# Two sums made one type earlier, and four reorderings, in a fused attention and feed-forward kernel

## The chip, the cores and the metric

One core of a Trainium2 chip. The time is the device time of one execution in microseconds; the lower the better. [...]

## The reference

```
q, k, v: (8 batches, 8 heads, 576 positions, 64); w_in: (512, 2048); w_out: (2048, 512)
attention within chunks of 64 positions:
    scores = q_c @ k_c^T / 8;  attn = softmax(scores);  out = attn @ v_c
x = out, as 4608 tokens x 512
h = x @ w_in                       # 4608 x 2048
g = h * tanh(softplus(h))          # "mish"
result = g @ w_out                 # 4608 x 512
```

## The kernel before

The 4608 tokens are 36 tiles of 128, that is 18 pairs of tiles. The first two pairs go through a plain version of the feed-forward part while the weights are read and split. The other sixteen pairs are worked in four rounds `m` = 1 to 4 of four pairs, with a Strassen-Winograd scheme: each product of two matrices, cut in 2 x 2 blocks, is made with seven block products instead of eight, and sums of blocks before and after. While round `m` is worked, the attention of the pairs of round `m` + 1 is done beside it. The whole order of instructions is written out by hand: each engine gets its instructions in the order in which the program emits them and works them in that order; semaphores hold an instruction back until its inputs are there and its output's buffer is free.

In rounds 1 and 2 the product with `w_in` uses the seven-product scheme (`unit`, eight units `u` of two blocks of 128 columns of h; in each unit the steps 0 to 7, behind each of which `beside` may put other work), and the product with `w_out` is the plain one (`down`; its products are held in a list and used as filling between, and in `phase_two` sixteen steps `f` of 12 products each work off the round's second half). In rounds 3 and 4 both products use the scheme.

For that, sums of blocks of w_out are built in round 2: the build of a unit has four steps, `t_whole` (VectorE puts the two parts of w_out together, line 210), `t_sums` (VectorE, three sums, line 219), `t_hi` (ScalarE, upper part, line 223) and `t_lo` (VectorE, lower part, line 227, and then the store to DRAM, which frees the buffer). All builds use one buffer, pool `c_p`, and so do copies of outputs on their way out (`ob_1b`, `ob_2a`, `ob_2b`). `t_keep` stores the blocks that need no sum. The dictionary `BUILDS_OUT` says behind which step of which unit each build step stands.

In rounds 3 and 4, `up_two(m, n)` makes two units at a time, `n` = 0 to 3, with 14 block products each (`product`, six matmuls of 512 columns, line 764), and behind each the function `beside(h)`, `h` = 0 to 13. ScalarE copies a product out of PSUM (lines 996, 1001, 1003), VectorE adds another (line 776), ScalarE applies mish (line 474). The result are the blocks G11, G12, G21, G22 of g for each unit. `s_sums(u)` makes S1 = G21 + G22 and S3 = G11 - G21 on VectorE (lines 943 and 944). Beside it the attention of one pair runs: scores on TensorE (line 271), maximum, difference, exponential, sum, inverse and normalisation on VectorE and ScalarE (lines 297 to 330), transposes on TensorE into PSUM (line 339), a copy of them by ScalarE (line 349), the values' product on TensorE (line 271 again) and its copy (line 360). Scores, transposes and values use one PSUM tile in turn.

`down_all(m)` is the second product: seven types `k` of products, one after the other, each over the eight units:

```
("G11", "W11", "X"), ("G12", "W21", "Y"), ("S2", "T2", "X"), ("S1", "T1", "Z"),
("S3", "T3", "X"), ("S4", "W22", "Z"), ("G22", "T4", "X")
```

The first name is the block of g, the second the block made of w_out, the third the PSUM tiles (two banks each) that take the sum. S2 = S1 - G11 and S4 = G12 - S2. One step, a pair (k, u), is 12 matmuls of 256 columns in `mine` (line 1060): four blocks of 128 tokens times three parts. Two steps ahead of it `operand(k, u)` is emitted: for S2 and S4 first the sum on VectorE (lines 1017 and 1020), in the place of G11 and G12; then the upper part `gh` on ScalarE (line 1024), and the lower part `gl` on VectorE (line 1026), which needs `gh`. `gh` and `gl` have three buffers each. Behind every other step stands one step of the split or sum of the next round's input (`x_step`, lines 415, 416 and 421) in round 3; round 4 has none. Behind a type's last unit the results are copied out of PSUM by ScalarE (`keep`, line 1075) or added by VectorE (`total`, line 1079). At step 1 stand the sums `s_sums` of the last two units, and in round 3 the values' product of the last pair. The blocks of the weights come from DRAM, 256 KB each, eleven in advance (`load_op`, line 751).

Of the kernel before, what the change touches and what calls it, by code (L numbers as in the profile page):

```python
# [14 lines left out]
ALU = mybir.AluOpType  # L15
# [8 lines left out]
def kernel(  # L24
# [22 lines left out]
    nc = tc.nc  # L47
# [5 lines left out]
    NU = NF // 2  # L53
# [338 lines left out]
    def first_pair(m):  # L392
        return PAIRS + 4 * (m - 1)
# [48 lines left out]
    def x_step(m, half, n):  # L442
        step = X_STEPS[n]
        if len(step) == 1:
            x_split(m, half, *step)
        else:
            x_sum(m, half, *step)
# [211 lines left out]
    def slot(s):  # L659
# [52 lines left out]
    BOTH_FROM = 3  # L712
# [11 lines left out]
    TYPES = (  # L724
        ("G11", "W11", "X"),
        ("G12", "W21", "Y"),
        ("S2", "T2", "X"),
        ("S1", "T1", "Z"),
        ("S3", "T3", "X"),
        ("S4", "W22", "Z"),  # L730
        ("G22", "T4", "X"),
    )
# [21 lines left out]
    def next_op():  # L754
        used.append(0)
        return wop[len(used) - 1]
# [29 lines left out]
        ):  # L786
            BUILDS.setdefault(place, []).append((step, n))
    BUILDS_OUT = {}
    for n, (u, h) in enumerate(((1, 0), (2, 0), (3, 0), (4, 0), (4, 4), (5, 0), (6, 0), (7, 0))):
        for i, step in enumerate((t_whole, t_sums, t_hi, t_lo)):  # L790
            BUILDS_OUT.setdefault((u, h + i), []).append((step, n))
        BUILDS_OUT.setdefault((n, 7), []).append((t_keep, n))

    def unit(m, u):
# [99 lines left out]
    def z_of(f):  # L894
        return zb[f // 8][:, f // 2 % 4, f % 2]

    def phase_two(m):
        after = m < QUADS
        p = first_pair(m)
        todo = []  # L900
        if after:
            todo = [lambda n=n: x_step(m + 1, 0, n) for n in range(len(X_STEPS))]
            todo += [lambda: a_raw(first_pair(m + 1) + 3)]
            todo += [lambda n=n: x_step(m + 1, 1, n) for n in range(len(X_STEPS))]
        for f in range(NF):
            d = {}
            if f == 0:
                filled(12)
            g_split(d, z_of(f), f"{m}b_{f}", True)
            if f == 0:  # L910
                for t in range(TOK // P):
                    filled(3)
                    store(f"{m}a", (p, p + 2), t)
            elif after or f < NF - 1:
                filled(12)
            down((m, 1), f, d)
            for _ in range(2):
                if todo:
                    todo.pop(0)()
            if f == 1 and m == 1:  # L920
                a_values(first_pair(m + 1) + 3)
            if f == 10 and m + 1 < QUADS:
                load_qk(first_pair(m + 2))
# [5 lines left out]
    G = {}  # L929
# [11 lines left out]
    def s_sums(u):  # L941
        s1, g11, g21, g22 = (G[u, n] for n in ("S1", "G11", "G21", "G22"))
        nc.vector.tensor_tensor(out=s1, in0=g21, in1=g22, op=ALU.add)
        nc.vector.tensor_tensor(out=g21, in0=g11, in1=g21, op=ALU.subtract)
        G[u, "S3"] = g21

    def up_two(m, n):
        units = (2 * n, 2 * n + 1)
        xt, yt, vt = flip(m)
        j = first_pair(m + 1) + n  # L950
        on = m < QUADS
        x, y, v_ = {}, {}, {}

        def beside(h):
            if h in (1, 2) and n:
                s_sums(2 * n - 3 + h)
            if not on:
                return
            if h == 1:
                a_scores(j)  # L960
                load_v(j)
            elif h == 2:
                a_max(j)
            elif h == 3:
                a_sub(j)
                if n < 3:
                    load_qk(j + 1, pool=(ob_p, "ob"))
            elif h == 4:
                a_exp(j)
            elif h == 6:  # L970
                a_inverse(j)
            elif h == 7:
                a_norm(j)
            elif h == 9:
                a_transpose(j)
                a_copy(j)
            elif h == 11 and n < 3:
                a_values(j)
                a_raw(j)

        for k in range(7):
            for i, u in enumerate(units):
                if k == 0:
                    x[u] = bank(f"x_{m}_{u}", xt[i])
                    z11 = z_new(m, u, "G11")
                    for name in ("G12", "G21", "G22", "S1"):
                        z_new(m, u, name)
                if k == 1:
                    y[u] = bank(f"y_{m}_{u}", yt[i])
                if k == 3:  # L990
                    v_[u] = bank(f"v_{m}_{u}", vt[i])
                o = y[u] if k == 1 else v_[u] if k in (3, 6) else x[u]
                product(k, o, k in (0, 1, 3))
                z = {name: G[u, name] for name in ("G11", "G12", "G21", "G22")}
                if k == 0:
                    nc.scalar.copy(out=z["G11"], in_=o)
                elif k == 1:
                    add(o, z["G11"])
                    mish(z["G11"], z["G11"])
                elif k == 2:  # L1000
                    nc.scalar.copy(out=z["G21"], in_=o)
                elif k == 4:
                    nc.scalar.copy(out=z["G22"], in_=o)  # L1003
                    add(v_[u], z["G22"])
                    mish(z["G22"], z["G22"])
                elif k == 5:
                    mish(z["G12"], o)
                elif k == 6:
                    add(o, z["G21"])
                    mish(z["G21"], z["G21"])  # L1010
                beside(2 * k + i)

    def operand(k, u):
        name = TYPES[k][0]
        if name == "S2":
            G[u, "S2"] = G[u, "G11"]
            nc.vector.tensor_tensor(out=G[u, "S2"], in0=G[u, "S1"], in1=G[u, "G11"], op=ALU.subtract)
        if name == "S4":
            G[u, "S4"] = G[u, "G12"]
            nc.vector.tensor_tensor(out=G[u, "S4"], in0=G[u, "G12"], in1=G[u, "S2"], op=ALU.subtract)  # L1020
        d = {}
        g = G[u, name]
        d["gh"] = ew_l.tile([P, TOK], F32R, name=f"gh_{k}_{u}", tag="gh")
        nc.scalar.copy(out=d["gh"], in_=g)  # L1024
        d["gl"] = ew_l.tile([P, TOK], F32R, name=f"gl_{k}_{u}", tag="gl")
        nc.vector.tensor_tensor(out=d["gl"], in0=g, in1=d["gh"].bitcast(F32), op=ALU.subtract)  # L1026
        return d
# [10 lines left out]
    def down_all(m):  # L1038
# [9 lines left out]
        banks_ = {}  # L1048
        ob = {}
        steps_ = [(k, u) for k in range(len(TYPES)) for u in range(NU)]  # L1050
        ready = [operand(*steps_[0]), operand(*steps_[1])]

        def mine(k, u, d, w_, bs=(0, 1)):
            acc_ = banks_[TYPES[k][2]]
            for t in (t for b in bs for t in (2 * b, 2 * b + 1)):
                o = acc_[t // 2][:, t % 2 * 256 : (t % 2 + 1) * 256]
                for n, (g, part) in enumerate((("gl", 0), ("gh", 1), ("gh", 0))):
                    nc.tensor.matmul(  # L1060
                        o,
                        lhsT=d[g][:, t * P : (t + 1) * P],
                        rhs=w_[:, part],
                        start=(k in (0, 1, 3) and u == 0 and t % 2 == 0 and n == 0),
                        stop=(u == NU - 1 and n == 2),
                        skip_group_check=True,
                    )
# [23 lines left out]
        for i, (k, u) in enumerate(steps_):  # L1091
            if u == 0 and k in (0, 1, 3):
                name = TYPES[k][2]
                banks_[name] = [bank(f"{name}_{m}_{b}", tags[name][b]) for b in range(2)]
            if i == 1:
                for u_ in (NU - 2, NU - 1):
                    s_sums(u_)
            if i + 2 < len(steps_):
                ready.append(operand(*steps_[i + 2]))
            w_ = next_op()  # L1100
            if last and k == len(TYPES) - 1 and u >= NU - 2:
                rest.append((k, u, ready.pop(0), w_))
            else:
                mine(k, u, ready.pop(0), w_)
            load_op()
            if i == 1 and not last:
                a_values(nxt + 3)
            if i % 2 and todo:
                todo.pop(0)()
            if u == NU - 1 and k in ends:  # L1110
                for b in range(2):
                    ends[k](b)
            if (k, u) == (6, 2) and m + 1 < QUADS:
                load_qk(first_pair(m + 2), pool=(ob_p, "ob"))
        ob["C21"] = ob_p.tile([P, 4, 256], F32, name=f"C21_{m}", tag="ob")
        for b in range(2):
            for r in rest:
                mine(*r, (b,))
            o = ob["C21"][:, 2 * b : 2 * b + 2]
# [74 lines left out]
```

## Time and profile before

| | |
|---|---|
| time, median of 3 runs | 892.27 us (892.26 to 895.66) |
| the profiled execution | 893.57 us, its span 891.8 us |
| mean granted clock of TensorE | 0.981 |
| TensorE matmuls busy | 823.5 us (92%) |
| VectorE busy | 525.3 us (59%) |
| ScalarE busy | 437.1 us (49%) |
| DMA, mean | 203 GB/s |

The stages in the profile's time: the first two pairs to about 160 us, round 1 to about 330, round 2 to 520 (its second half from 471), round 3 to 714 (its `down_all` from 614), round 4 to the end (its `down_all` from 791).

In the profile's rows PE is TensorE's matmuls and PEld its weight loads, DVE is VectorE, ACT ScalarE, SP SyncE; "L1026" is line 1026 of the kernel. A row of a timeline gives start and duration in us, engine, line, operation, output<-input, shapes and count, and in brackets the idle time before it on its engine and what ended that. A row of the chain that ended last gives start, duration, and what it was.

### The profile page before, as it was taken

What the parts mean: (1) busy time and instruction counts of PE and PEld (TensorE: products, weight loads), DVE (VectorE), ACT (ScalarE), POOL (GpSimd) and SP (SyncE); (2) the same over time, 40 slices, a digit from 0 to 9 for tenths busy, and PEclk for the clock granted to TensorE, in tenths of its full rate; (3) what the DMA queues carried; (4) which work ended last, traced back from release to release, by engine and by line L of the source; (5) the groups of instructions that cost most, each with busy time, mean ns of one, the idle gap of its engine ahead of it and who ended that gap; (6) DMA issues with size and microseconds to landing.
All of it is one profiled execution on the core that took longest, in us unless ns stands there. A gap on an engine that the chain in (4) does not pass through costs nothing.

```text
span 891.8 us, 15840 instructions
## 1 busy us (share of the span) xinstructions
PE 823.5 (92%) x6300; PEld 693.1 (78%) x6300; DVE 525.3 (59%) x765; ACT 437.1 (49%) x640; POOL 0.7 (0%) x6
## 2 busy tenths in 40 slices
PE   4979988889999999999999999998988999989987
PEld 4757866668888887787788887777878888879887
DVE  6788788556464645647666544455667623345554
ACT  4768766344354534445345435556454344434433
POOL 0000000000000000000000000000000000000000
PEclk9789999999999999999999999999999999989999
DMA  7788766775875306976975069664656676656562
GB/s 271 255 306 307 275 203 214 264 270 204 291 256 155 96 0 179 323 256 233 308 238 165 0 197 306 209 197 136 171 159 170 182 214 191 191 147 179 167 188 61
DMA packets 96440, 181.39 MB, mean 203 GB/s; under 512 B 9072, under 2 KB 29552, under 8 KB 94320
## 3 DMA queue, kind: packets, MB, share of 16 engines
q1 hardware_dynamic: 95936, 179.74, 63.5%
q8 instruction: 50, 0.82, 0.4%
q10 hardware_dynamic: 432, 0.66, 0.3%
q14 instruction: 22, 0.18, 0.1%
HBM read 137.36 MB, written 42.99 MB: 202 GB/s over the span
## 4 chain that ended last, share of the span: by engine, by line
PE 64%; DVE 17%; ACT 9%; DMA 5%; issue 3%; SPq 1%; ACTq 0%; DVEq 0%
PE x L764 15%; PE v L764 8%; PE X L1060 8%; PE y L764 4%; PE Z L1060 3%; DVE gl L1026 3%; ACT gh L1024 2%; DMA wst<-in_w_in 2%; PE av L271 2%; PE Y L1060 2%; DVE wc L132 2%; PE s L271 2%; PE pt L339 2%; PE o_(1, 1)_0_2761 L493 1%; PE o_(2, 1)_0_4421 L493 1%
## 5 line engine op out<-in xcount | busy, mean ns | idle before, releaser
L764 PE MATMUL x<-x_T,w 128*128 128x512 f32 x576 | 144.8, 394 | 5.9 <-ACT zb L868 3.3
L764 PEld LDWEIGHTS x<-x_T,w 128*128 128x128 f32 x576 | 106.1, 188 | 32.3 <-ACT zb L868 4.6
L1024 ACT CAST gh<-G 128x512 fp32r<-128x512 f32 x96 | 58.9, 619 | 96.0 <-PE X L1060 30.6
L1026 DVE TENSOR_TENSOR gl<-G,gh 128x512 fp32r<-128x512 f32 x96 | 65.8, 692 | 59.7 <-ACT gh L1024 58.6
L1060 PE MATMUL X<-w,gh 128*128 128x256 f32 x512 | 95.4, 287 | 0.0
L1060 PE MATMUL X<-w,gl 128*128 128x256 f32 x256 | 75.5, 295 | 14.6 <-DVE gl L1026 14.6
L1060 PEld LDWEIGHTS X<-w,gh 128*128 128x128 f32 x512 | 81.9, 197 | 0.0
L1060 PEld LDWEIGHTS X<-w,gl 128*128 128x128 f32 x256 | 50.3, 196 | 18.1 <-DVE gl L1026 18.1
L776 DVE TENSOR_TENSOR G<-v,G 128x512 f32<-128x512 f32 x32 | 22.1, 691 | 65.8 <-ACT G L1003 34.7
L474 ACT ACTIVATE G<-G 128x512 f32<-128x512 f32 x48 | 30.3, 632 | 59.5 <-DVE G L776 59.5
L461 PE MATMUL h<-x_first,wi 128*128 128x512 f32 (+1 forms) x204 | 50.6, 402 | 0.7 <-ACT x_first L379 0.7
L764 PE MATMUL v<-x_B,w 128*128 128x512 f32 x192 | 48.5, 395 | 2.5 <-DVE zb L776 2.5
L764 PE MATMUL v<-x_T,w 128*128 128x512 f32 x192 | 47.8, 391 | 2.4 <-DVE z L776 1.7
L764 PE MATMUL x<-x_B,w 128*128 128x512 f32 x192 | 48.6, 394 | 0.8 <-DVE x_B L416 0.8
L764 PE MATMUL y<-x_B,w 128*128 128x512 f32 x192 | 49.1, 397 | 0.0
L474 ACT ACTIVATE zb<-zb 128x512 f32<-128x512 f32 x32 | 20.2, 632 | 57.2 <-DVE zb L776 57.2
L1060 PE MATMUL Z<-w,gh 128*128 128x256 f32 x256 | 47.9, 287 | 0.0
L461 PEld LDWEIGHTS h<-x_first,wi 128*128 128x128 f32 x204 | 39.4, 207 | 9.0 <-ACT x_first L379 0.9
L1060 PE MATMUL Z<-w,gl 128*128 128x256 f32 x128 | 38.3, 299 | 8.0 <-DVE gl L1026 7.9
L764 PEld LDWEIGHTS v<-x_B,w 128*128 128x128 f32 x192 | 35.4, 188 | 11.6 <-DVE zb L776 4.2
L764 PEld LDWEIGHTS v<-x_T,w 128*128 128x128 f32 x192 | 35.8, 188 | 10.9 <-DVE z L776 2.1
L493 PE MATMUL o<-wo,gh 128*128 128x512 f32 x128 | 42.5, 414 | 0.3 <-DVE wo L153 0.3
(181 smaller groups left out, 1614.6 us busy)
## 6 DMA issues: line engine op xcount, KB each, us to landing
w<-wa SPq DMA_DIRECT2D x224, 256.0 KB, 3.2
w<-wb SPq DMA_DIRECT2D x112, 256.0 KB, 2.8
v<-in_v SPq DMA_DIRECT2D x16, 512.0 KB, 5.9
wa<-a SPq DMA_DIRECT2D x8, 1024.0 KB, 4.1
wb<-t SPq DMA_DIRECT2D x8, 1024.0 KB, 4.5
wst<-in_w_out SPq DMA_DIRECT2D x7, 1024.0 KB, 5.5
wst<-in_w_in SPq DMA_DIRECT2D x6, 1024.0 KB, 6.1
wa<-wi SPq DMA_DIRECT2D x24, 256.0 KB, 3.9
```

Of the source, the lines that this page charges most:

```text
L132: nc.vector.scalar_tensor_tensor(out=c, in0=x, scalar=mask, in1=y, op0=op, op1=ALU.bitwise_or)
L271: nc.tensor.matmul(o[h * CHUNK : (h + 1) * CHUNK, c, t - ts.start, g], lhsT=l[rows, t, 2 * g + h], rhs=r[rows, t, 2 * g + h], start=True, ...
L339: nc.tensor.transpose(out=d["pt", ts.start][:, t - ts.start, g], in_=d["p"][:, t, g].rearrange("p c k -> p (c k)"), identity=ident,)
L461: nc.tensor.matmul(h[:, cols], lhsT=wi[i // 2][:, i % 2, w_, kt], rhs=x[:, x_, kt, cols], start=(n == 0), stop=(n == 3 * NK - 1),)
L474: nc.scalar.activation(out=out_, in_=in_, func=AF.Mish)
L493: nc.tensor.matmul(acc[t], lhsT=g[:, t * P : (t + 1) * P], rhs=wo[:, f, part], start=(f == 0 and n == 0), stop=(f == NF - 1 and n == 2),)
L764: nc.tensor.matmul(o, lhsT=t[:, w_, kt], rhs=x[x_][:, kt], start=(start and i == 0), stop=(i == 5), skip_group_check=not start,)
L776: nc.vector.tensor_tensor(out=z, in0=o, in1=z, op=ALU.add)
L1024: nc.scalar.copy(out=d["gh"], in_=g)
L1026: nc.vector.tensor_tensor(out=d["gl"], in0=g, in1=d["gh"].bitcast(F32), op=ALU.subtract)
L1060: nc.tensor.matmul(o, lhsT=d[g][:, t * P : (t + 1) * P], rhs=w_[:, part], start=(k in (0, 1, 3) and u == 0 and t % 2 == 0 and n == 0), sto ...
```

## The change

Five edits:

- The sums S2 and S4 leave `operand`. S2 of unit u is made behind `operand` of step (1, u), S4 behind that of step (3, u), by the new function `difference`: one type ahead of the type that uses them.
- In `mine`, the three parts become the outer loop and the four blocks of tokens the inner one, and the order of parts changes: first the four upper x lower, then the four upper x upper, last the four products with the lower part `gl`.
- The operands of the first two steps of `down_all` are emitted behind products 10 and 11 of the last pair of units in `up_two`, not at the start of `down_all`; the list `ready` moves out of `down_all` for that.
- In `up_two`, the attention's transposes and their copy move from behind product 9 to behind product 10, the values' product and its copy from 11 to 12.
- In round 2, unit n + 1 has the build of unit n, one in each unit; before, unit 4 had two builds, and units 5 to 7 those of units 5 to 7. The build of unit 7 moves into `phase_two`, steps 6 to 9.

```diff
--- before.py
+++ after.py
@@ -786,9 +786,10 @@
         ):
             BUILDS.setdefault(place, []).append((step, n))
     BUILDS_OUT = {}
-    for n, (u, h) in enumerate(((1, 0), (2, 0), (3, 0), (4, 0), (4, 4), (5, 0), (6, 0), (7, 0))):
-        for i, step in enumerate((t_whole, t_sums, t_hi, t_lo)):
-            BUILDS_OUT.setdefault((u, h + i), []).append((step, n))
+    T_STEPS = (t_whole, t_sums, t_hi, t_lo)
+    for n in range(NU):
+        for i, step in enumerate(T_STEPS if n < NU - 1 else ()):
+            BUILDS_OUT.setdefault((n + 1, i), []).append((step, n))
         BUILDS_OUT.setdefault((n, 7), []).append((t_keep, n))
 
     def unit(m, u):
@@ -917,6 +918,8 @@
             for _ in range(2):
                 if todo:
                     todo.pop(0)()
+            if m == BOTH_FROM - 1 and 0 <= f - 6 < len(T_STEPS):
+                T_STEPS[f - 6](NU - 1)
             if f == 1 and m == 1:
                 a_values(first_pair(m + 1) + 3)
             if f == 10 and m + 1 < QUADS:
@@ -954,6 +957,8 @@
         def beside(h):
             if h in (1, 2) and n:
                 s_sums(2 * n - 3 + h)
+            if h in (10, 11) and n == NU // 2 - 1:
+                ready.append(operand(0, h - 10))
             if not on:
                 return
             if h == 1:
@@ -971,10 +976,10 @@
                 a_inverse(j)
             elif h == 7:
                 a_norm(j)
-            elif h == 9:
+            elif h == 10:
                 a_transpose(j)
                 a_copy(j)
-            elif h == 11 and n < 3:
+            elif h == 12 and n < 3:
                 a_values(j)
                 a_raw(j)
 
@@ -1010,16 +1015,15 @@
                     mish(z["G21"], z["G21"])
                 beside(2 * k + i)
 
+    ready = []
+
+    def difference(u, out_, x, y):
+        G[u, out_] = G[u, "G11" if out_ == "S2" else "G12"]
+        nc.vector.tensor_tensor(out=G[u, out_], in0=G[u, x], in1=G[u, y], op=ALU.subtract)
+
     def operand(k, u):
-        name = TYPES[k][0]
-        if name == "S2":
-            G[u, "S2"] = G[u, "G11"]
-            nc.vector.tensor_tensor(out=G[u, "S2"], in0=G[u, "S1"], in1=G[u, "G11"], op=ALU.subtract)
-        if name == "S4":
-            G[u, "S4"] = G[u, "G12"]
-            nc.vector.tensor_tensor(out=G[u, "S4"], in0=G[u, "G12"], in1=G[u, "S2"], op=ALU.subtract)
         d = {}
-        g = G[u, name]
+        g = G[u, TYPES[k][0]]
         d["gh"] = ew_l.tile([P, TOK], F32R, name=f"gh_{k}_{u}", tag="gh")
         nc.scalar.copy(out=d["gh"], in_=g)
         d["gl"] = ew_l.tile([P, TOK], F32R, name=f"gl_{k}_{u}", tag="gl")
@@ -1048,15 +1052,14 @@
         banks_ = {}
         ob = {}
         steps_ = [(k, u) for k in range(len(TYPES)) for u in range(NU)]
-        ready = [operand(*steps_[0]), operand(*steps_[1])]
 
 
 
         def mine(k, u, d, w_, bs=(0, 1)):
             acc_ = banks_[TYPES[k][2]]
-            for t in (t for b in bs for t in (2 * b, 2 * b + 1)):
-                o = acc_[t // 2][:, t % 2 * 256 : (t % 2 + 1) * 256]
-                for n, (g, part) in enumerate((("gl", 0), ("gh", 1), ("gh", 0))):
+            for n, (g, part) in enumerate((("gh", 1), ("gh", 0), ("gl", 0))):
+                for t in (t for b in bs for t in (2 * b, 2 * b + 1)):
+                    o = acc_[t // 2][:, t % 2 * 256 : (t % 2 + 1) * 256]
                     nc.tensor.matmul(
                         o,
                         lhsT=d[g][:, t * P : (t + 1) * P],
@@ -1097,6 +1100,10 @@
                     s_sums(u_)
             if i + 2 < len(steps_):
                 ready.append(operand(*steps_[i + 2]))
+            if k == 1:
+                difference(u, "S2", "S1", "G11")
+            elif k == 3:
+                difference(u, "S4", "G12", "S2")
             w_ = next_op()
             if last and k == len(TYPES) - 1 and u >= NU - 2:
                 rest.append((k, u, ready.pop(0), w_))
```

## The prediction

> **What bounds the kernel now.** I read the page's busy times first, then the kernel cut into stretches, then the chain of work that ended last from the third round on, and last the queues of VectorE and ScalarE inside the stretches where TensorE waits.
>
> ```profile
> PE 823.5 (92%) x6300; PEld 693.1 (78%) x6300; DVE 525.3 (59%) x765; ACT 437.1 (49%) x640; POOL 0.7 (0%) x6
> ...
> core 0: us, PE busy (x) PEld busy (x) DVE busy (x) ACT busy (x) POOL busy (x), PEclk, DMA share, GB/s
> 628.50:640.10 11.60, 11.60 (x99) 11.60 (x99) 7.86 (x12) 5.68 (x10) 0.00 (x0) 1.00 0.66 183
> 714.04:790.70 76.66, 76.66 (x337) 62.43 (x335) 24.08 (x36) 31.70 (x55) 0.00 (x0) 1.00 0.70 199
> 790.70:805.00 14.30, 11.62 (x74) 11.63 (x75) 8.55 (x13) 5.30 (x10) 0.00 (x0) 0.76 0.39 112
> ```
>
> TensorE is the bound: 92% busy, and in whole stretches (714 to 791 us) never idle, with the DMA share at 0.70 and the clock at 1.00. So a gain can only come from the stretches where TensorE waits. The chain shows where these are:
>
> ```profile
> 611.48 2.73 PE v L764 x12
> ...
> 616.88 3.14 PE X L1060 x24
> 620.01 1.09 PE av L271 x64
> ...
> 660.32 11.52 PE Z L1060 x96
> ...
> 702.52 11.52 PE X L1060 x96
> 714.04 2.75 PE x L764 x12
> ...
> 787.98 2.73 PE v L764 x12
> ...
> 793.38 14.47 PE X L1060 x96
> ...
> 836.10 11.52 PE Z L1060 x96
> ...
> 875.60 11.53 PE X L1060 x96
> ```
>
> These are the two passes of the second product (`down_all`), seven types of 96 products each. An undisturbed type takes 11.52 us, so one product 0.12 us and a step of 12 products 1.44 us; seven types are 80.64 us. The third round's pass runs from the end of the last first product (611.48 + 2.73 = 614.21) to 714.04: 99.83 us, which is 80.64, the attention's 1.09, and 18.1 lost. The fourth's runs from 790.71 to 887.13 (875.60 + 11.53): 96.42 us, 15.8 lost. Inside: at each start 2.67 us in which TensorE does nothing (614.21 to 616.88, 790.71 to 793.38); 2.95 us in the fourth's first type (14.47 instead of 11.52); and in three types each time 616.88 to 660.32 (43.44 - 34.56 - 1.09 = 7.8), 660.32 to 702.52 (42.20 - 34.56 = 7.6), 793.38 to 836.10 (42.72 - 34.56 - 2.95 = 5.2) and 836.10 to 875.60 (39.50 - 34.56 = 4.9). These four, 25.5 us, lie in the third and the sixth type, S2 and S4. Why:
>
> ```profile
> 649.66 0.68 DVE L1017 TENSOR_TENSOR G<-S,G 128x512 f32<-128x512 f32 x1
> 650.46 0.62 ACT L1024 CAST gh<-G 128x512 fp32r<-128x512 f32 x1 [1.52 <-DVE G L1017]
> 651.11 0.69 DVE L1026 TENSOR_TENSOR gl<-G,gh 128x512 fp32r<-128x512 f32 x1 [0.76 <-ACT gh L1024]
> 651.72 0.68 DVE L1017 TENSOR_TENSOR G<-S,G 128x512 f32<-128x512 f32 x1
> 651.86 0.39 PE L1060 MATMUL X<-w,gl 128*128 128x256 f32 x1 [0.97 <-DVE gl L1026]
> ```
>
> The reader is to see a closed ring: the sum on VectorE (649.66), the upper part on ScalarE that waits for it (650.46), the lower part on VectorE that waits for that (651.11), and only then the next sum (651.72). One turn is 651.72 - 649.66 = 2.06 us, above a step's 1.44. VectorE is not full; it waits 0.76 us in each turn.
>
> **Part 1: the sums one type ahead.** 16 sums of 0.68 us per pass move from the third and sixth types into the second and fourth. None is added. The ring breaks: an upper part then waits only for its buffer (three in turn). What is late next is VectorE's queue itself in the types that take the sums, above all in the third round, where it also splits the next round's input.
>
> ```profile
> 629.25 1.31 ACT L1075 COPY P<-X 128x512 f32<-128x512 f32 x2
> 643.15 0.68 DVE L416 TENSOR_TENSOR x_T<-raw,x_T 128x512 fp32r<-128x512 f32 x1
> 643.75 1.28 DVE L1079 TENSOR_TENSOR P<-Y,P 128x512 f32<-128x512 f32 x2
> 644.95 0.68 DVE L1017 TENSOR_TENSOR G<-S,G 128x512 f32<-128x512 f32 x1
> ```
>
> Back to back, three VectorE operations take 644.95 - 643.15 = 1.80 us, 0.60 to 0.61 each though each is listed at 0.68. In the second type of the third round VectorE gets 8 lower parts, 8 sums and 4 input operations, then two totals and the lower part of the third type's third step: 23 x 0.61 = 14.0 us. It starts some 1.8 us into the type, after the two copies (1.31) and one upper part (0.62, less overlap). Ready: 15.8 us from the type's start. Needed, with part 2, two thirds into that step: 10 x 1.44 + 0.96 = 15.36. So some 0.5 us late, and with restart I charge 0.7; at 0.69 us each it is 17.7, so 2.3 late. The fourth type has no totals: 21 x 0.61 + 1.8 = 14.6 against 15.36, nothing (0.9 late at 0.69). The fourth round has no input operations: 19 x 0.61 + 1.8 = 13.4, nothing.
>
> **Part 2: the lower parts' products last.** The same 12 products and 12 weight loads per step, reordered. Gain: a lower part may come 8 x 0.12 = 0.96 us later, and an upper part's buffer is free 0.48 us earlier. Cost: bank and moving operand now alternate otherwise. Rows show no price for it: the 628.50 to 640.10 stretch changes region every three products and bank every six, at 1.00 clock and 11.52 us a type. I charge nothing; the far bounds are under the rivals.
>
> **Part 3: the first splits moved into the last pair.** Two upper and two lower parts go behind products 10 and 11 of the last pair, where ScalarE and VectorE have room (31.70 and 24.08 of 76.66 us in the fourth round). The chain product, addition, mish, upper part, lower part (2.67 us) leaves both starts, and the third step's parts take its place later. Behind it stand the last four sums of S1 and S3 on VectorE:
>
> ```profile
> 617.94 0.68 DVE L943 TENSOR_TENSOR S<-G,G 128x512 f32<-128x512 f32 x1
> 620.60 0.68 DVE L1026 TENSOR_TENSOR gl<-G,gh 128x512 fp32r<-128x512 f32 x1
> ```
>
> Four sums take 2.66 us. From the pass's start the third lower part begins at about 1.95 us (the gap's 2.67 less a lower part's 0.69), the sums follow it, and the fourth is ready at 1.95 + 0.61 + 2.66 + 0.68 = 5.9. TensorE needs it at 3 x 1.44 + 0.96 = 5.28: 0.7 us late in the fourth round, 0.9 with restart. In the third round the attention's 1.09 us and its load gap stand before it, so nothing.
>
> The 2.95 us of the fourth's first type: its 96 products ran while the granted clock was 0.76, right after the 2.67 us gap; the equal gap at 614.21 cost no clock (11.52 us types follow). I take it that the gap brings it and that it goes. [...]
>
> So the third round's pass gains 18.1 - 0.7 = 17.4 us, the fourth's 15.8 - 0.9 = 14.9.
>
> **Part 4: one build per unit (second round).**
>
> ```profile
> 369.92 1.59 PE y L764 x6
> ...
> 403.37 1.60 PE y L764 x6
> ...
> 441.05 1.59 PE y L764 x6
> ...
> 413.78 1.23 DVE L210 TENSOR_TENSOR t<-wo 128x1024 f32<-128x1024 f32 x1 [1.57 <-DMA wb<-t]
> 425.20 1.22 DVE L210 TENSOR_TENSOR t<-wo 128x1024 f32<-128x1024 f32 x1 [4.14 <-DMA wb<-t]
> 415.66 1.67 PE L764 MATMUL v<-x_B,w 128*128 128x512 f32 x6 [1.18 <-DVE zb L776]
> 428.73 1.67 PE L764 MATMUL v<-x_T,w 128*128 128x512 f32 x6 [1.69 <-DVE z L776]
> ```
>
> A build's first step waits for the store of the build before (one buffer), and everything behind it on VectorE waits too, until TensorE does (1.69 at 428.73). Units three and four take 403.37 - 369.92 = 33.45 us, five and six 441.05 - 403.37 = 37.68. With one build each they should take the same: 4.2 gained (2.9 if only the two named waits of TensorE, 1.18 and 1.69, go). The last build moves into the second half, steps 6 to 9:
>
> ```profile
> 491.26 0.69 DVE L483 TENSOR_TENSOR gl_2b<-zb,gh_2b 128x512 fp32r<-128x512 f32 x1 [1.42 <-ACT gh_2b L479]
> 496.70 0.69 DVE L483 TENSOR_TENSOR gl_2b<-zb,gh_2b 128x512 fp32r<-128x512 f32 x1 [0.82 <-ACT gh_2b L479]
> 416.65 1.61 DVE L219 TENSOR_TENSOR t<-t 128x512 f32<-128x512 f32 x3
> ```
>
> There a step is 2.72 us (two in 496.70 - 491.26) with some 0.8 us idle on VectorE. The build adds 1.22, 1.61, 0 and 1.22 us to four steps. Stepping through from 491.26: a lower part and two splits (3 x 0.61), 1.2, a lower part, a split and a sum (3 x 0.61), 1.6, and the lower part of step 8 begins at 497.6 instead of 496.70. There it had some 1.9 us to spare (a step less the upper part before it); it needs 0.69, and now has 1.0. Nothing charged; were that 0.3 us of cover gone, some 0.5. Its store goes to SyncE's queue with its data ready, and the buffer's next user, the output copies at the half's end, comes six steps later. In the second round's units six to eight the builds only change their number.
>
> **Part 5: attention one product later (third round).**
>
> ```profile
> 559.56 1.07 PE L339 MATMUL pt<-ident,p 128*128 128x128 f32 x8 [0.98 <-DVE p L330]
> 560.59 0.57 ACT L1003 COPY G<-x 128x512 f32<-128x512 f32 x1
> 563.49 1.02 PEld L271 LDWEIGHTS av<-ps,v 64*64 64x64 f32 x64 [0.54 <-ACT ps L349]
> ```
>
> The transposes no longer wait 0.98 us, but the product after them needs the bank that the copy at 560.59 empties (to 561.16): it starts at 561.2 instead of 561.74. So 0.5 us per pair, not 1, and about 0.3 at the values' product. Pairs two and three gain 0.8, pair four 0.5 (its values' product lies in the next pass), and pair one, whose transposes did not wait, an estimate of 0.4 to 0.6; less 0.2 for the splits put before the last copy: 2.4 us. Bounds: 0, if the copies only hand the wait on, and 4 x 0.98 = 3.9.
>
> **Sum.** 4.2 + 2.4 + 17.4 + 14.9 = 38.9 us off the profiled execution's 893.57 (span 891.8): 854.7. The median of the runs shown, 892.27, is 1.3 below it; on that level 853.4, and I say 854.
>
> **Rivals.**
> - *The wait only moves.* VectorE's ring forms again where the sums now stand: all 25.5 us stay, 893.57 - 13.4 = 880, some 879 on the median's level. For it: VectorE gets 20 operations in 11.5 us. Against it: no sum stands any more between an upper part and its lower part's step, and the totals above. Its mild form, the 0.69 us bound, adds 1.6 + 0.9: 857.
> - *The clock stays low in the fourth round's first type*: 2.95 more, 857. For it: only one of two gaps lowered it.
> - *The reordered products run slower* (the other side). Place: 2 x 672 = 1344 products. Each has to lose 38.9 / 1344 = 29 ns before the change gains nothing. Price: at the 0.76 clock 96 products took 14.47 us, 31 ns more each, 41 us in all: 895. Against: the 11.52 us types already alternate banks at clock 1.00. [...]
>
> **Chances.** Forecast 0.73; the wait moves 0.12; clock stays 0.10; slower products 0.05, of which 0.02 within 0.5% and 0.03 beyond (about what a measurement of this kernel can tell from no change). All others are faster by over 0.5%: 0.95. Range: down to 850 (nothing of the charged 1.6 us, 2 more from attention), up to 863 (both bounds of VectorE, the clock, no gain in attention). It leaves out the far end of the first rival and the slower products.
>
> **What would show it.** S2 and S4 types of 11.5 us; no idle time before either pass's first product, and a granted clock of 1.00 behind it; TensorE's waits for lower parts, now at every turn of the ring, under 3 us in all and left at the third type of the third round and the fourth step of the fourth; units five and six at 33.5 us; transposes without a wait, the product behind them with about 0.5. Wrong would be me if VectorE's waits for upper parts come back in the second and fourth types, or if undisturbed types take more than 11.52 us.

## The result and the profile after

The changed kernel takes 854.34 us (median; 853.87 to 855.94), the kernel before 893.96 in the same comparison: 0.9555 of its time, 95% interval 0.9519 to 0.9591. The forecast was 854. The profiled execution's span is 852.8 us instead of 891.8, 39.0 less; the sum said 38.9.

In the rows below, `gh` is the upper part of a float32 operand and `gl`, the rest of it, the lower part, both of type `float32r` ("fp32r" in the rows); a product is the sum of lower x upper, upper x lower and upper x upper, added in PSUM.

The page's busy row and the chain of the kernel after (start, duration, what), with two rows of TensorE's timeline for the end of the third round's first product, which the chain leaves out:

```profile
PE 810.4 (95%) x6300; PEld 686.4 (80%) x6300; DVE 521.6 (61%) x765; ACT 436.1 (51%) x640; POOL 0.7 (0%) x6
...
402.76 1.59 PE y L764 x6
...
436.22 1.59 PE y L764 x6
...
515.66 2.72 PE x L764 x12
...
643.71 11.52 PE Z L1063 x96
655.23 11.52 PE X L1063 x96
666.75 11.52 PE Z L1063 x96
678.27 11.52 PE X L1063 x96
689.79 2.75 PE x L764 x12
...
763.71 2.72 PE v L764 x12
766.43 1.45 PE X L1063 x12
...
772.53 6.49 PE X L1063 x52
779.03 11.52 PE Y L1063 x96
...
836.63 11.53 PE X L1063 x96
```

```profile
603.99 2.91 PE L764 MATMUL v<-x_B,w 128*128 128x512 f32 x12
606.73 1.12 PE L1063 MATMUL X<-w,gh 128*128 128x256 f32 x8
```

The types S2 and S4 are now as long as the others, but for 0.3 us at the third round's S2 (11.83 us): from 643.71 on, four types in a row in the third round take 11.52 us each, and from 779.03 on all of the fourth. The second product begins with no gap, at the end of the product before it: at 603.99 + 2.91 = 606.90 in the third round (the row at 606.73 begins 0.17 us ahead of the end of the row before it) and at 766.43 in the fourth. It takes 689.79 - 606.90 = 82.9 us in the third round instead of 99.83 and 848.16 - 766.43 = 81.7 in the fourth instead of 96.42; 80.64 (and 1.09 for the values' product in the third) is the floor. Units five and six of the second round take 436.22 - 402.76 = 33.46 us.

| part | forecast | before | after | gained |
|---|---|---|---|---|
| units five and six, round 2 | 4.2 | 37.68 | 33.46 | 4.2 |
| first product, round 3 (to 614.21 / 606.90) | 2.4 | 93.72 | 91.24 | 2.5 |
| second product, round 3 | 17.4 | 99.83 | 82.89 | 16.9 |
| second product, round 4 | 14.9 | 96.42 | 81.73 | 14.7 |
| all else | 0 | | | 0.7 |

The 93.72 and the 91.24 us begin where the two chains have the round's first products, at 520.49 and 515.66. Of the last row, 0.6 us lie ahead of the fifth unit (403.37 and 402.76), in the part that no edit touches; that part differs by some 5 us between the profiles below (401.33 to 406.23).

### The profile page after: what moved, and what is told of

Its sections match the earlier page's. It is cut to its first block, busy times and chain, and to the rows that moved or that the text cites. A ratio compares the mean times of both kernels' runs of the same rounds, so it can differ in the third digit from the quotient of the medians.

```text
span 852.8 us, 15933 instructions
## 1 busy us (share of the span) xinstructions
PE 810.4 (95%) x6300; PEld 686.4 (80%) x6300; DVE 521.6 (61%) x765; ACT 436.1 (51%) x640; POOL 0.7 (0%) x6
## 4 chain that ended last, share of the span: by engine, by line
PE 76%; DVE 10%; DMA 5%; ACT 5%; issue 2%; SPq 1%; DVEq 0%; ACTq 0%
PE x L764 17%; PE X L1063 9%; PE v L764 9%; PE Z L1063 5%; PE y L764 5%; PE av L271 2%; DMA wst<-in_w_in 2%; PE s L271 2%; PE h L461 2%; PE o L493 2%; PE pt L339 2%; DVE wc L132 1%; PE Y L1063 1%; PE o_(1, 1)_0_2761 L493 1%; PE o_(2, 1)_0_4413 L493 1%
## 5 line engine op out<-in xcount | busy, mean ns | idle before, releaser
L1063 PE MATMUL X<-w,gh 128*128 128x256 f32 x512 | 72.3, 283 | 0.0
L1063 PEld LDWEIGHTS X<-w,gh 128*128 128x128 f32 x512 | 66.3, 192 | 0.2
L1063 PE MATMUL X<-w,gl 128*128 128x256 f32 x256 | 41.8, 284 | 1.3 <-DVE gl L1030 1.2
L764 PEld LDWEIGHTS x<-x_B,w 128*128 128x128 f32 x192 | 35.2, 188 | 8.6 <-DVE x_B L416 1.2
L764 PEld LDWEIGHTS y<-x_B,w 128*128 128x128 f32 x192 | 35.1, 188 | 7.7
L481 DVE CAST gh<-z 128x512 fp32r<-128x512 f32 x40 | 16.9, 423 | 39.7 <-PE o_(2, 0)_3_3328 L493 20.6
```

What stands on the lines that cost most here:

```text
L481: nc.vector.tensor_copy(out=d["gh"], in_=z)
L764: nc.tensor.matmul(o, lhsT=t[:, w_, kt], rhs=x[x_][:, kt], start=(start and i == 0), stop=(i == 5), skip_group_check=not start,)
L1063: nc.tensor.matmul(o, lhsT=d[g][:, t * P : (t + 1) * P], rhs=w_[:, part], start=(k in (0, 1, 3) and u == 0 and t % 2 == 0 and n == 0), sto ...
```

## The experiments

Since that first part varies, each profile is also read from the start of the fifth unit's second product (the chain's row "PE y") to the end of the span. All five edits lie behind it. Each row is one profile.

| kernel | fifth unit | span | from there | against the change |
|---|---|---|---|---|
| before | 403.37 | 891.8 | 488.4 | +38.4 |
| the change | 402.76 | 852.8 | 450.0 | |
| sums_alone | 403.58 | 868.0 | 464.4 | +14.4 |
| all_but_sums | 402.41 | 872.1 | 469.7 | +19.7 |
| old_order | 401.66 | 854.6 | 452.9 | +2.9 |
| late_first_splits | 402.74 | 857.0 | 454.3 | +4.2 |
| first_splits_alone | 402.04 | 884.8 | 482.8 | +32.7 |
| old_builds | 402.29 | 856.5 | 454.2 | +4.2 |
| old_attention | 403.60 | 855.5 | 451.9 | +1.9 |
| banks_in_turn | 406.23 | 856.4 | 450.2 | +0.1 |
| later_last_sums | 401.33 | 849.6 | 448.3 | -1.8 |
| combined | 404.72 | 851.7 | 447.0 | -3.1 |

**sums_alone: the sums one type ahead, nothing else.**

```diff
 # on the kernel before
-        if name == "S2": ... if name == "S4": ...      (in operand)
+            if k == 1:
+                difference(u, "S2", "S1", "G11")
+            elif k == 3:
+                difference(u, "S4", "G12", "S2")
```

> The kernel before, with S2 and S4 made one type ahead and nothing else of the change. Theory (the ring of sum, upper part, lower part caused the 25.5 us in the third and sixth types, and making the sums ahead opens it): these types take 11.5 us each but for a start up to 1.5 us late in the third round's third type, since the lower part is still needed at a step's first product; 2.67 us stay at both starts of the second product, and the fourth round's first type may stay at 14.5 us; in all some 24 us faster, 869 to 871 us. Rival (the sums need the reordered products as well, because VectorE's queue is full in the types that take them): at most 15 us faster, 879 us or more, with waits for lower parts spread over the second and fourth types of the third round.

Measured 869.38 us, 0.9733 of before (0.9683 to 0.9783); 24.0 us less from the fifth unit on. The ring was the cause, and the sums do not need the reordering. Its chain in the fourth round, and two of its stretches with the granted clock (third column from the right):

```profile
779.80 14.47 PE X L1057 x96
...
805.79 11.52 PE X L1057 x96
...
840.35 11.52 PE Z L1057 x96
```

```profile
777.20:779.80 2.60, 0.00 (x0) 0.00 (x0) 1.40 (x3) 1.91 (x4) 0.00 (x0) 0.88 0.61 184
779.80:786.00 6.20, 6.20 (x29) 6.20 (x30) 4.36 (x8) 1.50 (x3) 0.00 (x0) 0.50 0.16 42
```

S2 (805.79) and S4 (840.35) are undisturbed; the gap and the slow first type behind it stay, at a clock of 0.50 for 6 us. In the third round S2 still takes 12.53 us: its start comes 1.0 us late, within the 1.5 that were allowed for it.

**all_but_sums: the change without its sums.**

```diff
 # on the changed kernel
+        if name == "S2": ... if name == "S4": ...      (in operand again)
-            if k == 1: difference(...)  elif k == 3: difference(...)
```

> The changed kernel, with the sums S2 and S4 back in front of the upper part two steps ahead; all else of the change stays. Theory: the ring is back, one turn of 2.06 us (2.66 with an input operation) against a step of 1.44; the reordered products give back some 0.96 us in each of the four types that have it; the third and sixth types take 15 to 18 us each, and the kernel is 21 to 25 us slower than the changed one: 876 to 880 us. Rival (the reordering of products alone hides most of the ring): under 10 us slower, below 865 us.

Measured 875.05 us, 0.9792 (0.9741 to 0.9843), and 19.7 us more than the change from the fifth unit on: the theory's side, a little under its range. The ring comes back, but the reordering makes it cheaper by more than the 0.96 us per type that I gave it: its chain

```profile
620.01 6.73 PE Y L1070 x56
647.49 1.70 PE X L1070 x12
649.19 11.52 PE Z L1070 x96
```

has S2 from 631.53 (620.01 + 11.52) to 649.19, 17.7 us, 6.1 lost where the kernel before, from 641.46 to 660.32, lost 7.3. That is 1.2 us less. TensorE now waits there for the upper part, not the lower one (from 600 to 700 us, 4.6 us in six waits for `gh` in the types on X, 0.5 in one for `gl`); that the earlier release of its buffer (0.48 us) makes up the rest is argued, not shown.

**old_order: the change with the old order of products in a step.**

```diff
-            for n, (g, part) in enumerate((("gh", 1), ("gh", 0), ("gl", 0))):
-                for t in (...):
+            for t in (...):
+                for n, (g, part) in enumerate((("gl", 0), ("gh", 1), ("gh", 0))):
```

> The changed kernel, with the products of a step in the old order (block of tokens outside; lower, upper x lower, upper x upper inside). Theory: the new order gives each lower part 0.96 us, which is used only where VectorE is late: the fourth step of either round's first type and the start of the third round's third type; each of these waits becomes some 0.96 us longer, 2.9 us in all: 857 us. An undisturbed type takes 11.52 us in both orders. Rival one: the order matters at every step (the later release of an upper part's buffer makes ScalarE late): 5 us or more slower, 860 us. Rival two: the new order costs TensorE something itself; then undisturbed types are shorter than 11.52 us here.

Measured 857.29 us, 0.959 (0.9549 to 0.9632), 2.9 us more from the fifth unit on: as forecast in sum. TensorE's waits in the third round, fourth step and third type, in its timeline:

```profile
612.77 0.39 PE L1063 MATMUL X<-w,gl 128*128 128x256 f32 x1 [1.42 <-DVE gl L1030]
635.38 0.39 PE L1063 MATMUL X<-w,gl 128*128 128x256 f32 x1 [0.76 <-DVE gl L1030]
```

In the changed kernel the first is 0.41 and the second too short to be listed; the one at the fourth round's fourth step is 1.56 us here and 0.83 there. The parts were not quite as forecast: both first types grow by 1.0 us, the third round's third type by only 0.7, and its fifth type, for which nothing was forecast, by 0.3. Undisturbed types are 11.52 us here too, so the new order costs TensorE nothing.

**late_first_splits and first_splits_alone: the first two operands at the start again, and only this part of the change.**

```diff
 # late_first_splits, on the changed kernel (first_splits_alone: the reverse, on the kernel before)
-            if h in (10, 11) and n == NU // 2 - 1:
-                ready.append(operand(0, h - 10))
+        ready.extend(operand(*s) for s in steps_[:2])      # in down_all
```

> The changed kernel, with the first two operands emitted at the start of the second product, as before. Theory: TensorE waits at both starts for addition, mish and upper part, some 2.0 us each (no longer for the lower part), in return the fourth step's waits (0.6 and 0.8 us) mostly go, since the chain ahead of them is the same; 2.5 to 3 us slower, and if a gap of 2 us lets the granted clock fall, up to 3 us more in the first type after it: 857 to 860 us. Rival (the start's wait was hidden anyway by later waits): within 1 us of the changed kernel.

> The kernel before, with the first two operands behind products 10 and 11 of the last pair and nothing else of the change. Theory (the 2.67 us gap at the start of the fourth round's second product lets the granted clock fall): no gap at either start, and the fourth round's first type shows a clock of 1.00 and loses nothing but a wait of some 1.8 us at its fourth step (the lower part is still needed first); some 6 us faster than before, 886 to 888 us, the ring in the third and sixth types unchanged. Rival (the clock falls for another reason, at that time or place): the first type still takes 14 us or more besides that wait.

The first: 858.55 us, 0.9597 (0.9555 to 0.964), and 4.2 us more from the fifth unit on. These are two gaps of 1.95 us and one fall of the clock, 1.5 us (the third round's first type takes 14.55 us; in the kernel before, with no fall there, 13.06), less the two waits at the fourth step, which are gone. Its stretches at both starts:

```profile
606.80:608.80 2.00, 0.09 (x1) 0.00 (x0) 0.69 (x1) 1.27 (x4) 0.00 (x0) 1.00 0.60 189
608.80:613.50 4.70, 4.66 (x28) 4.49 (x32) 4.61 (x8) 2.79 (x5) 0.00 (x0) 0.64 0.27 81
769.40:771.40 2.00, 0.06 (x1) 0.00 (x0) 0.70 (x2) 1.27 (x4) 0.00 (x0) 1.00 0.74 186
771.40:776.00 4.60, 4.59 (x38) 4.59 (x39) 4.53 (x8) 2.70 (x5) 0.00 (x0) 1.00 0.35 95
```

Two equal gaps: behind the third round's the clock falls to 0.64, behind the fourth's it stays at 1.00. In the kernel before it was the other way round, 1.00 behind the third round's (616.90 to 620.00) and 0.53 behind the fourth's (793.40 to 800.00); why was not shown. The second kernel, a single run, took 886.55 us, 5.7 us less than before from the fifth unit on, as forecast. Its fourth round:

```profile
788.00:802.00 14.00, 12.43 (x102) 12.06 (x101) 8.29 (x13) 7.30 (x13) 0.00 (x0) 1.00 0.54 160
```

The gap gone, the clock is 1.00 at that place with the rest of the kernel as before. The rival, another reason at that time or place, falls. In the kernel before, the clock falls in one more of these types, the third round's S4:

```profile
640.10:660.32 20.22, 14.68 (x110) 13.26 (x109) 14.50 (x23) 8.71 (x16) 0.00 (x0) 1.00 0.53 153
...
683.40:702.52 19.12, 14.52 (x98) 13.18 (x98) 13.50 (x23) 7.45 (x13) 0.00 (x0) 0.91 0.54 148
```

S4, at 0.91, takes 19.16 us there, and S2 (from 641.46), at 1.00, 18.86; in first_splits_alone they take 19.13 and 18.87. Even with the clock at 0.91 TensorE is idle for 4.60 of the 19.12 us: the ring sets the pace, not TensorE.

**old_builds: the builds where they were.**

```diff
-    for n in range(NU): ... (n + 1, i)        and T_STEPS in phase_two
+    for n, (u, h) in enumerate(((1, 0), (2, 0), (3, 0), (4, 0), (4, 4), (5, 0), (6, 0), (7, 0))): ...
```

> The changed kernel, with the builds where they were before (two in unit 4, the last in unit 7). Theory: VectorE waits again for the store of the build before, units five and six of the second round take 37.7 us instead of 33.5, nothing is gained in the second half of the round: 4.2 us slower, 858 to 859 us. Rival (the build in the second half costs what the second unit's build cost): no difference to the changed kernel, 854 us.

Measured 858.27 us, 0.9598 (0.9569 to 0.9627); 4.2 us more from the fifth unit on. Its chain has the fifth and the seventh unit at

```profile
402.29 1.60 PE y L764 x6
...
439.95 1.59 PE y L764 x6
```

37.66 us, as before the change. The last build costs nothing in the second half.

**old_attention: transposes behind product 9, values behind 11.**

```diff
-            elif h == 10:               (a_transpose, a_copy)
+            elif h == 9:
-            elif h == 12 and n < 3:     (a_values, a_raw)
+            elif h == 11 and n < 3:
```

> The changed kernel, with transposes and values' product of the third round one product earlier, as before. Theory: the wait of some 1 us at the transposes comes back in pairs two to four, and 0.5 us of waits behind them go: 2 to 2.7 us slower, 856 to 857 us. Rival one (the wait moves entirely, from the transposes to the product behind them): no difference. Rival two: the full 1.4 us per pair comes back, over 4 us slower.

Measured 855.95 us, 0.9571 (0.9541 to 0.9601); 1.9 us more from the fifth unit on, just under the forecast of 2 to 2.7. TensorE's waits in its first product of the third round (in total, times, longest), and those of the changed kernel:

```profile
PE pt L339 <- DVE p L330: 2.9, 3, 1.0
PE av L271 <- ACT ps L349: 0.4, 1, 0.4
```

```profile
PE x L764 <- ACT G L1008: 1.1, 3, 0.4
```

Three waits of 1.0 us turn into three of 0.4 one product later: part of the wait moves on, as the sum had it. The first product is 2.4 us longer here, but in the third round the wait at the fourth step of the second product is gone, 0.5 us, which brings the net to 1.9.

**banks_in_turn: another PSUM bank at every product.**

```diff
-                for t in (t for b in bs for t in (2 * b, 2 * b + 1)):
+                for t in (2 * b + c for c in (0, 1) for b in bs):
```

> The changed kernel, with the four blocks of tokens of a step in the order 0, 2, 1, 3 instead of 0, 1, 2, 3, so that every product of the second product goes to another PSUM bank than the one ahead of it. Theory (a change of bank costs TensorE nothing): types of 11.52 us, granted clock 1.00, 854 us. Rival (alternating between banks costs issue time or clock, which the new order already pays in part): types longer than 11.52 us; at the 31 ns of the low clock per product 41 us slower, and a cost of 2 ns per product would already show as 11.7 us a type.

Measured 856.2 us, 0.9566 (0.953 to 0.9601), and 0.1 us more from the fifth unit on, with its types at

```profile
794.14 11.52 PE X L1063 x96
805.66 11.52 PE Z L1063 x96
```

With a change of bank at every product 96 of them take 11.52 us as well; no cost shows. The slower rival has no ground here: an undisturbed type takes 11.52 us in every order and with every change of bank that was run.

**later_last_sums: the last four sums behind steps 3 and 5.**

```diff
-            if i == 1:
-                for u_ in (NU - 2, NU - 1):
-                    s_sums(u_)
+            if i in (3, 5):
+                s_sums(NU - 2 + (i == 5))
```

> The changed kernel, with the sums S1 and S3 of the last two units behind steps 3 and 5 of the second product instead of both at step 1. Theory: the wait of the fourth step (0.6 us in the third round, 0.8 in the fourth, with restart) goes, since the fourth lower part no longer stands behind four sums (2.66 us); two sums later cost nothing, as VectorE has over 0.7 us to spare in a step of the first type: 1.2 to 1.6 us faster than the changed kernel. Rival (VectorE's backlog only moves on to the second type, where the sums S2 stand): the third type's start in the third round becomes later by as much, and the gain is under 0.8 us.

Measured 852.3 us, 0.9538 (0.951 to 0.9567); 1.8 us less than the change from the fifth unit on, a little more than forecast. The wait at the fourth step is gone in both rounds, and the fourth round's second product is at its floor:

```profile
764.32 11.51 PE X L1063 x96
775.83 11.52 PE Y L1063 x96
...
833.43 11.53 PE X L1063 x96
```

844.96 - 764.32 = 80.64 us.

**combined: that, the first operands behind products 0 and 1, and the normalisation one product later.**

```diff
 # on later_last_sums
-            if h in (10, 11) and n == NU // 2 - 1:      (the first two operands)
+            if h in (0, 1) and n == NU // 2 - 1:
-            elif h == 7:                                (a_norm)
+            elif h == 8:
```

> The changed kernel, with the last two units' sums behind steps 3 and 5, the first two operands already behind products 0 and 1 of the last pair, and the attention's normalisation one product later (8 instead of 7). Theory: in the third round the additions of the last pair no longer stand behind a lower part that waits for ScalarE, the bank that the product behind the transposes needs is emptied some 1 us earlier, and the wait there (0.36 us each) and at the values' product goes, against a new wait of some 0.3 us at the transposes: 0.3 to 0.5 us per pair, 1 to 2 us faster than with the later sums alone, 850 to 851.5 us. Rival (the normalisation after the addition makes the transposes late by as much as it saves): the same as with the later sums alone, 852 us.

Measured 853.1 us, 0.9555 (0.9536 to 0.9574); from the fifth unit on 1.3 us less than with the later sums alone, as the theory said for that stretch, and the waits list none of TensorE's products behind another engine from the third round on. The whole time does not show it: this profile's fifth unit began 3.4 us later than the other's, in the part that both share. Neither this kernel nor later_last_sums is shown to be faster than the change by their intervals; in the stretch that the edits touch they are 3.1 and 1.8 us shorter, in one profile each. Which of the two edits that come on top gives the 1.3 us was not tried.

## Why the prediction was right

**The sum.** 38.9 us forecast and 39.0 measured is closer than the parts were. The second products gained 0.5 and 0.2 us less than forecast, the first product 0.1 more, and 0.7 came from where nothing was changed. That the errors cancel is luck; that each part came within 0.5 us, and at the place that was named, is not.

**Sums ahead.** The ring was the loss and its opening the gain: 24.0 us alone, forecast as 25.5 less a late start. One reading was off: 0.45 of the 25.5 us lay in the third round's first type (13.06 us before, where 11.52 and the attention's 1.09 make 12.61), not in the ring, and stayed. The working of VectorE's queue in the third round's second type is borne out almost row by row:

```profile
621.78 0.69 DVE L1030 TENSOR_TENSOR gl<-G,gh 128x512 fp32r<-128x512 f32 x1 [1.36 <-ACT gh L1028]
622.39 0.69 DVE L1022 TENSOR_TENSOR G<-S,G 128x512 f32<-128x512 f32 x1
...
633.84 1.28 DVE L1082 TENSOR_TENSOR P<-Y,P 128x512 f32<-128x512 f32 x2
635.03 1.28 DVE L1030 TENSOR_TENSOR gl<-G,gh 128x512 fp32r<-128x512 f32 x2
```

```profile
635.76 0.74 PE L1063 MATMUL X<-w,gl 128*128 128x256 f32 x4
```

From 621.78 to 635.03 VectorE does 22 operations without a pause, 0.60 us each (0.61 was taken, not the listed 0.68). The lower part is ready at about 635.72, and TensorE takes it up at 635.76 instead of some 635.56 (eight products after 634.60): 0.2 us late, where 0.7 was charged, 0.5 and my estimate of 0.2 for the restart. The type took 0.31 us more than an undisturbed one. The size was a little off, the place right.

**The fourth step.** Forecast: 0.7 us late in the fourth round, nothing in the third. The fourth round's wait is 0.83 us (the last row below). But the third round has one too, 0.41, and here a step failed: "In the third round the attention's 1.09 us and its load gap stand before it, so nothing".

```profile
604.71 1.02 ACT L349 COPY ps<-pt 128x1024 f32<-128x1024 f32 x1
606.10 0.63 ACT L1028 CAST gh<-G 128x512 fp32r<-128x512 f32 x1
606.76 0.69 DVE L1030 TENSOR_TENSOR gl<-G,gh 128x512 fp32r<-128x512 f32 x1 [1.23 <-ACT gh L1028]
607.37 1.28 DVE L776 TENSOR_TENSOR G<-v,G 128x512 f32<-128x512 f32 x2
609.85 0.69 DVE L1030 TENSOR_TENSOR gl<-G,gh 128x512 fp32r<-128x512 f32 x1 [1.21 <-ACT gh L1028]
613.86 0.74 PE L1063 MATMUL X<-w,gl 128*128 128x256 f32 x4 [0.41 <-DVE gl L1030]
...
772.53 0.74 PE L1063 MATMUL X<-w,gl 128*128 128x256 f32 x4 [0.83 <-DVE gl L1030]
```

The second early lower part (606.76) waits for its upper part, which on ScalarE stands behind the attention's copy (604.71), and the last pair's additions stand behind it on VectorE: they run at 607.37, both late. So the third lower part begins 2.95 us after the start (609.85 - 606.90), not 1.95, and the four sums come after that. In the fourth round, which has no attention, it begins after 2.1 us (768.53 - 766.43). I had charged ScalarE for the moved splits but not asked what is queued behind them on VectorE. old_attention, with the copy one product earlier, has no such wait; later_last_sums takes it away by moving the sums.

**Clock.** The 2.95 us of the fourth round's first type went with the gap: that place has a clock of 1.00 without the gap (first_splits_alone) and the same 14.47 us with it (sums_alone). The rival that it stays falls. But a gap alone does not do it: in late_first_splits that place has a gap of 1.95 us and a clock of 1.00. The prediction had seen that only one of two equal gaps lowered the clock, and had no reason for it; the runs show none either. In the profile before it was the fourth round's gap, in late_first_splits the third's, and these 2.95 us of the gain rest on that.

**Builds.** 4.2 forecast, 4.2 measured. The last build fits into the second half as stepped through, the tightest lower part beginning right behind the build's step of 1.60 us:

```profile
491.19 1.60 DVE L219 TENSOR_TENSOR t<-t 128x512 f32<-128x512 f32 x3
492.70 0.68 DVE L483 TENSOR_TENSOR gl_2b<-zb,gh_2b 128x512 fp32r<-128x512 f32 x1
```

It has no idle time before it, so it comes as early as VectorE can, and TensorE's waits from 331 to 516 us (0.3 and 0.2 us, both behind ScalarE) list none for it.

**Attention.** 2.4 forecast, 2.5 measured in the first product, by pair 0.5, 0.75, 0.7 and 0.5 us where 0.5, 0.8, 0.8 and 0.3 were forecast; the new wait of 0.36 to 0.37 us stands at the product that was named, and for the reason named (the bank emptied late).

**Reordering.** Nothing charged, nothing lost; its worth, 2.9 us beside the other edits, is what lets VectorE's late lower parts pass.

## What to carry to other kernels

When two engines hand work to each other and back, and the first has to finish one turn before it starts the next, count the turn of that ring (here 2.06 us against a step of 1.44), not the engine's share of busy time: VectorE was 59% busy, and the wait came from its own order. Work that depends on nothing late can be put a whole stage ahead, if the queue it is put into is added up to its deadline with the back-to-back spacing (0.60 us), not the listed duration (0.68). And for each instruction that is moved, look at what stands behind it on the engine that waits for it, not only on the one that does it.

## What the runs showed of the hardware

Six starts of the second product have an idle gap of TensorE of 1.95 us or more: two each in the kernel before, sums_alone and late_first_splits. Behind three of them the granted clock was lower, and the first type took longer: 14.55 us instead of 13.06 in the third round of late_first_splits, 14.47 instead of 11.52 in the fourth of the other two. The two gaps of the kernel before and the stretches behind them (the first number behind the comma is TensorE's busy time, the third from the right the clock):

```profile
614.20:616.90 2.70, 0.02 (x1) 0.03 (x1) 1.46 (x3) 1.97 (x5) 0.00 (x0) 1.00 0.62 182
616.90:620.00 3.10, 3.10 (x28) 2.97 (x29) 3.03 (x6) 1.38 (x3) 0.00 (x0) 1.00 0.13 24
...
790.70:793.40 2.70, 0.03 (x1) 0.03 (x1) 1.46 (x3) 1.97 (x5) 0.00 (x0) 0.87 0.54 185
793.40:800.00 6.60, 6.60 (x32) 6.60 (x33) 4.76 (x8) 1.47 (x3) 0.00 (x0) 0.53 0.19 43
800.00:805.00 5.00, 5.00 (x44) 5.00 (x43) 2.33 (x4) 1.86 (x3) 0.00 (x0) 1.00 0.59 163
```

| gap from | length | stretch behind it | clock in that stretch |
|---|---|---|---|
| before, 614.20 | 2.68 | 616.90 to 620.00 | 1.00 |
| before, 790.70 | 2.68 | 793.40 to 800.00 | 0.53 |
| sums_alone, 614.30 | 2.68 | 617.00 to 620.00 | 1.00 |
| sums_alone, 777.12 | 2.68 | 779.80 to 786.00 | 0.50 |
| late_first_splits, 606.89 | 1.95 | 608.80 to 613.50 | 0.64 |
| late_first_splits, 769.46 | 1.95 | 771.40 to 776.00 | 1.00 |

In each of the three kernels the two gaps are equally long and only one has a lower clock behind it, so the length of a gap alone does not tell what follows. In the kernel before and in sums_alone the clock was below 1.00 within the gap already (0.87 from 790.70 to 793.40, 0.88 from 777.20 to 779.80). What decides between two equal gaps was not shown.
